# Sparse attention and a squared-ReLU feed-forward on one core: transposing on TensorE instead of in the DMA queues

## The chip, the cores and the metric

The kernel runs on one core of a Trainium2 chip. The metric is the device time of one execution in microseconds; the time of before is the median of three runs.

## The reference

Inputs are `q`, `k`, `v` of 8 batches x 8 heads x 576 tokens x 64, all float32, and two weights. Cut to what matters:

```python
scores = (q @ k.transpose(0, 1, 3, 2)) / sqrt(64)
rel = pos[:, None] - pos[None, :]
mask_local   = (rel >= 0) & (rel < 32)                    # heads 0 to 3
mask_strided = (rel >= 0) & (pos_k % 32 == pos_q % 32)    # heads 4 to 7
attn = softmax(where(mask, scores, -1e9))
x = (attn @ v).transpose(0, 2, 1, 3).reshape(4608, 512)
h = x @ w_in                                              # 512 -> 2048
g = s * relu(h)**2 + b
out = g @ w_out                                           # 2048 -> 512, float32
```

## The kernel before, in words

**Attention.** Heads are worked on in pairs: a batch `b` has four pairs `m`, 0 and 1 of the band (local) heads, 2 and 3 of the strided ones. A pair stands on the 128 partitions as two heads of 64. Band heads are cut in `LT` = 6 tiles of `LQ` = 96 queries, each with a window of 128 keys. Strided heads are cut by residue in `ST` = 8 groups of `SQ` = 72 tokens. For each pair `pair_steps` makes these steps: transposes of queries and keys (`trans`, L527 and L535), so that the 64 features lie on partitions; scores (`score`, L656); exponentials on ACT and a mask on DVE; the product with the values (`av`, L717), whose last column gives the sum; a division on DVE into `x_nat`; and a transpose of the outputs (`xtrans`, L764) into `xT`, from which the feed-forward reads.

Transposes are made in two ways. On TensorE a transpose is a matmul against the identity into a PSUM bank, and ACT or DVE copies the bank out (all these copies are recorded at L437, `copy_on`). In batches 0 and 1 (`HEAD_T` = 2) the band heads are transposed singly (L527): two matmuls of 64 columns of weights, one head into PSUM partitions 0 to 63, the other into 64 to 127. In batches 2 to 4 `pair_post` first copies two heads of the loaded queries or keys next to each other (`qp`, `kp`), and one matmul of 128 columns of weights (L535) takes both. Strided heads lie side by side as loaded and always go as a pair. The other way is a transposing DMA on SP's queue: strided keys from batch 3 (`k_dma`), band keys from `KB_DMA` = 4, strided queries from `QS_DMA` = 3, band queries from `QB_DMA` = 5 (`q_dma`; `q_spread` then copies the queries apart), band outputs from batch 2 (`x_dma`), strided outputs from `XS_DMA` = 4 through a buffer in DRAM (`x_out`, `x_in`).

**Feed-forward.** The 4608 tokens are cut in 9 blocks `T` of 512. `ff1` (L1016) multiplies a block with `w_in`; ACT takes the ReLU, ACT or DVE the square. `ff2` (L1271) multiplies with `w_out`. From block 2 on the second product is done with seven instead of eight block products (`ff2_seven`, L984), in the last two blocks the first one too (`ff1_seven`, L1241). `L1526` is filler that keeps TensorE running in the head.

**Order.** The order on every engine is written out when the program is made. `Plan` keeps a clock in ns. A `Step` on TensorE has a reckoned cost (`ns`: 40 for a position of single heads, 35 for another transpose or an `av`, 216 for a 512-column matmul), keys that it needs, and work that it posts to ACT, DVE, POOL or the queues. `flush` picks among posted work by the time at which it was ready plus a priority from `ORDER`, which here has four sets, changed at the times in `UNTIL`. The main loop takes an attention step when it is ready and due, else a step of `ff1` or `ff2`.

**Banks.** PSUM has eight banks: `t` (transposes, 1), `s` (scores, 2), `a` (attention outputs, 1), `f1` and `f2` (feed-forward, 2 each). `group_of` says which banks a fill may take; from batch `KB_DMA` on, `a` may also use `t`.

**Loads.** `fetch_qk(b)` has POOL issue the loads of queries and keys of a batch, `fetch_v(b)` those of the values. In `fetch_qk` POOL first copies one element of the transposed strided keys of batch b-1 to `gate` (L1356), so that it waits until that transposing DMA has landed. From `QB_DMA` and `KB_DMA` on band queries and keys are loaded head by head (L387). `landing` reckons when a load will be there.

Of the kernel before, what the change touches and what calls it, by code (L numbers as in the profile page):

```python
# [139 lines left out]
class Step:  # L140
    def __init__(self, fn, ns, needs=(), group=None, keys=(), posts=(), after=None):
# [4 lines left out]
UNTIL = (26000.0, 110000.0, 215000.0)  # L146
ORDER = [
    {"g": 0.0, "S": -2500.0, "in": 500.0, "w_mix": 2500.0, "wc": 0.0, "ev": 2500.0, "c21": -200.0,
     "c11": 2500.0, "c12": 200.0, "C22": 1500.0, "fv": -200.0, "Vb": 0.0, "x": 500.0, "Ub": 500.0,
     "xc": 500.0, "fe": -400.0, "k": -400.0, "fu": 200.0, "Va": 500.0, "p": 1000.0, "c22": -800.0,  # L150
     "Ua": -200.0, "e": -1500.0, "q": 500.0, "r": -800.0, "u": -2500.0, "SLACK": 200.0,
     "ahead": 0.0, "p2": -800.0, "r3": 500.0, "inkl0": 2500.0, "q3": 1000.0, "lead": 0.9,
     "r1": 2500.0, "k2": 2500.0, "x0": 0.0, "invs0": -400.0, "x2": 1500.0, "k0": 200.0,
     "inql1": 1000.0, "k3": -200.0, "q0": 1000.0, "q2": 2500.0, "p3": 2500.0, "inql0": 200.0,
     "r0": -2500.0, "invs1": 200.0, "p0": -1500.0, "r2": -200.0, "invl1": -2500.0, "x3": -200.0,
     "q1": 2500.0, "invl0": 2500.0, "k1": 0.0, "inkl1": -1500.0, "p1": 1000.0, "x1": 2500.0},
    {"g": -1500.0, "S": -400.0, "in": 2500.0, "w_mix": 200.0, "wc": -800.0, "ev": -200.0,
     "c21": 2500.0, "c11": -1500.0, "c12": -2500.0, "C22": 1500.0, "fv": -1500.0, "Vb": 2500.0,
     "x": 0.0, "Ub": 500.0, "xc": 200.0, "fe": 500.0, "k": -800.0, "fu": 1000.0, "Va": 500.0,
     "p": -200.0, "c22": 0.0, "Ua": 2500.0, "e": -1500.0, "q": -2500.0, "r": 1500.0, "u": -2500.0,  # L160
     "SLACK": 600.0, "ahead": -0.2, "r3": -200.0, "k1": 1500.0, "q1": -200.0, "invl1": -800.0,
     "x2": -800.0, "x3": -2500.0, "lead": 1.1, "k3": 0.0, "p1": 0.0, "inql0": 2500.0,
     "r0": -1500.0, "r2": -400.0, "invs0": 1000.0, "k0": -400.0, "q3": 0.0, "invl0": 1500.0,
     "p2": 2500.0, "x1": 500.0, "invs1": -200.0, "inkl0": 500.0, "inql1": 0.0, "q0": 1500.0,
     "k2": -2500.0, "inkl1": -2500.0, "p0": 500.0, "q2": -200.0, "p3": 0.0, "x0": 1000.0,
     "r1": -2500.0},
    {"g": 1500.0, "S": 2500.0, "in": 500.0, "w_mix": -800.0, "wc": 1000.0, "ev": 1000.0,
     "c21": -1500.0, "c11": 2500.0, "c12": 1000.0, "C22": 1000.0, "fv": -1500.0, "Vb": -200.0,
     "x": -400.0, "Ub": 200.0, "xc": -1500.0, "fe": -1500.0, "k": 500.0, "fu": 2500.0,
     "Va": 500.0, "p": 200.0, "c22": 200.0, "Ua": -400.0, "e": 1500.0, "q": 1000.0, "r": 1500.0,  # L170
     "u": 1500.0, "SLACK": 600.0, "ahead": -0.05, "lead": 1.1, "k1": -400.0, "inkl0": -400.0,
     "p2": 2500.0, "q0": 1000.0, "inql1": 1500.0, "x0": -200.0, "inql0": 2500.0, "q3": 1000.0,
     "invs0": 1000.0, "invl1": -800.0, "p0": 200.0, "k0": -1500.0, "r1": 1000.0, "inkl1": 0.0,
     "k3": 1000.0, "q1": -1500.0, "x2": -400.0, "invs1": 0.0, "x1": 200.0, "x3": 1000.0,
     "p3": 200.0, "p1": 2500.0, "k2": -400.0, "r3": 2500.0, "r2": 1500.0, "invl0": 1500.0,
     "q2": 1500.0, "r0": 2500.0},
    {"g": 200.0, "S": 200.0, "in": 200.0, "w_mix": 200.0, "wc": 1500.0, "ev": 1500.0,
     "c21": -400.0, "c11": -2500.0, "c12": -400.0, "C22": 200.0, "fv": -400.0, "Vb": -200.0,
     "x": -1500.0, "Ub": -400.0, "xc": 0.0, "fe": 0.0, "k": -200.0, "fu": -2500.0, "Va": -200.0,
     "p": -1500.0, "c22": 200.0, "Ua": 0.0, "e": -200.0, "q": 2500.0, "r": 200.0, "u": -1500.0,  # L180
     "SLACK": 1000.0, "ahead": -0.05, "q0": 1500.0, "q1": 500.0, "invs1": -400.0, "x1": -800.0,
     "q3": -400.0, "p2": -2500.0, "q2": 2500.0, "p1": -800.0, "p3": 0.0, "k1": -2500.0,
     "r2": -1500.0, "x3": -800.0, "inql1": 500.0, "invl1": -400.0, "x0": 1500.0, "inkl1": 500.0,
     "inkl0": 200.0, "inql0": -1500.0, "k0": 200.0, "r3": -2500.0, "r1": -2500.0, "k3": -1500.0,
     "invl0": -1500.0, "x2": -2500.0, "invs0": -2500.0, "k2": 200.0, "lead": 0.9, "p0": 1500.0,
     "r0": -2500.0},
]
# [34 lines left out]
def lay_out(ctx, tc, nc, q, k, v, moe_w_in, moe_w_out, moe_s, moe_b, out, order, q_shape, out_shape,  # L222
# [15 lines left out]
    SQ, ST = 72, 8  # L238
# [77 lines left out]
    QB_DMA, KB_DMA, QS_DMA, XS_DMA = 5, 4, 3, 4  # L316
    x_dram = [tc.dram_tile([S, 128], FP16, name=f"x_dram{i}") for i in range(4)]
# [52 lines left out]
    paired = {}  # L370

    def load_qk(b):
# [7 lines left out]
        for name, src in (("q", q), ("k", k)) if b else ():  # L380
            tl = inp.tile([LQ, NL], FP16, tag=name + "l", name=name + "l")
            loaded[b, name + "l"] = tl
            if b >= (QB_DMA if name == "q" else KB_DMA):

                dst = tl.rearrange("p (m t e d) -> p m e t d", m=2, t=LT, e=2)
                for h in range(4):
                    nc.gpsimd.dma_start(out=dst[:, h // 2, h % 2],  # L387
                                        in_=src[b, h].rearrange("(t p) d -> p t d", p=LQ))
            else:
                nc.gpsimd.dma_start(out=h4(tl), in_=view_l(src, b))  # L390
        for name, src in (("q", q), ("k", k)):
            if name == "k":
                ts = ks[b % 2]
            elif b < QS_DMA + 2:
                ts = inp.tile([SR, NS], FP16, tag="qs", name="qs")
            else:
                ts = loaded[b - 2, "qs"]
            if name == "k" and b in (2, 3) or name == "q" and b in (QS_DMA, QS_DMA + 1):
                nc.sync.dma_start(out=ts[SQ:SR], in_=h_zero.ap())
            load_s(ts, src, b)  # L400
            loaded[b, name + "s"] = ts
# [37 lines left out]
    def pair_post(b, name, mm, key):  # L439

        if (b, name) not in paired:
            paired[b, name] = None

        def g(eng):
            if paired[b, name] is None:
                paired[b, name] = inp.tile([128, 2, LT, 2 * D], FP16, tag="pp", bufs=3,
                                           name=name + "p")[0:LQ]
            from_ = loaded[b, name + "l"]
            copy_on(eng, out=paired[b, name][:, mm].rearrange("p j (e d) -> p e j d", e=2),
                    in_=from_.rearrange("p (m e j d) -> p m e j d", m=2, e=2, d=D)[:, mm])  # L450
        plan.post([key], {"A": 810, "V": 350}, g,
                  [("in", name + "l", b, mm)])

# [26 lines left out]
    HEAD_T = 2  # L480
    PE_MASK = 1
# [4 lines left out]
    def group_of(kind, b, m, q=False):  # L486
# [5 lines left out]
        elif b == 1 and kind == "a":  # L492
            banks = f1 + a
        elif b >= KB_DMA and kind == "a":
            banks = a + t
        elif b == 1 and q:
            banks = t + f2
        elif b == 2 and q:
            banks = t + f1
        elif kind == "t" and b == 1:  # L500
            banks = t + f1 + a
# [5 lines left out]
    def pair_steps(b, m):  # L507
# [10 lines left out]
        def trans(name, j, group):  # L518
            alone = loc and b < HEAD_T

            def f():
                if j == 0:
                    st["p" + name] = bank(group).bitcast(FP16)[:, 0:S]
                if alone:
                    for e in range(2):
# [7 lines left out]
                src = (paired[b, name][:, mm, j] if loc else  # L533
                       loaded[b, name + sfx][0:SQ, 1024 * mm + j * 128:1024 * mm + j * 128 + 128])
# [40 lines left out]
        k_by_dma = b >= (KB_DMA if loc else 3)  # L575
        q_by_dma = b >= (QB_DMA if loc else QS_DMA)
        x_by_dma = b >= 2 if loc else XS_DMA <= b

        def k_dma(eng):
            if loc:  # L580
                st["k"] = kT_loc[mm]
                if b > KB_DMA and (b - KB_DMA) % 2:

                    if b == KB_DMA + 1:
                        loaded["kT", mm] = qkp.tile([128, ST * SR], FP16, tag="kTs", name="kT_alt")
                        nc.gpsimd.memset(loaded["kT", mm][:, 0:LPAD], 0.0)
                    st["k"] = loaded["kT", mm]
                nc.sync.dma_start_transpose(
                    out=st["k"][:, LPAD:LPAD + S].rearrange("d (t p) -> d t p", t=nt),
                    in_=loaded[b, "kl"][:, 768 * mm:768 * mm + 768])  # L590
                return
            if b < KB_DMA:
                st["k"] = qkp.tile([128, ST, SR], FP16, tag="kTs", name="kTs")
            else:
                if (b, "kT2") not in loaded:
                    loaded[b, "kT2"] = inp.tile([128, 2, ST, SR], FP16, tag="vs", name="kT2")
                st["k"] = loaded[b, "kT2"][:, mm]
# [1040 lines left out]
```

## Time and profile before

| | |
|---|---|
| median of three runs | 297.5 us (297.36 to 298.87) |
| profiled execution, its own time | 297.4 us |
| span of its instructions | 295.5 us |
| TensorE (PE) busy, matmuls | 289.5 us, 2803 |
| weight loads (PEld) busy | 219.3 us |
| DVE busy | 236.8 us |
| ACT busy | 194.6 us |
| POOL busy | 92.8 us |
| mean DMA rate | 129 GB/s |
| granted TensorE clock | 1.000 |

Busy is the time in which at least one instruction of the engine is under way. A matmul's record is longer than the distance to the next start, since matmuls are pipelined: what a matmul costs a full TensorE is read from start to start. In a line of the timeline the columns are start and length in us, engine, line, operation, out<-in, `weights rows*columns`, shape of the output and type, and how many instructions are merged. In a line of the stages each engine has its busy time and, in brackets, its instructions; then come the granted clock, the DMA share and GB/s.

### The profile page before, as it was taken

The page shows a single profiled execution, that of the slowest core. Times are in us where ns is not written, and L with a number is a line of the kernel's source. Part 1 is how long each engine was busy: PE and PEld are TensorE (multiplying, and loading weights), DVE is VectorE, ACT ScalarE, POOL GpSimd, SP SyncE. Part 2 cuts the span into 40 slices and gives each one's busy share as a digit, 9 for nine tenths or more (in the row PEclk, how much of TensorE's full clock was granted, in tenths as well). Part 3 has the DMA queues.
Part 4 walks back from the last instruction along what each step waited for, and adds up shares of the span by engine and source line. Part 5 has one row for each costly group of instructions (what it writes and reads, how often), then busy time and mean ns, then how long its engine had stood idle before and what let it go on. Part 6 is the DMA issues. An engine that isn't in the chain of part 4 may idle for free.

```text
span 295.5 us, 7106 instructions
## 1 busy us (share of the span) xinstructions
PE 289.5 (98%) x2803; PEld 219.3 (74%) x2803; DVE 236.8 (80%) x498; ACT 194.6 (66%) x334; POOL 92.8 (31%) x140
## 2 busy tenths in 40 slices
PE   7899999999999999999999999999999999999995
PEld 3775655665565567989867785779888999999984
DVE  5765977888976789768986888688899689888874
ACT  3667855897967797947873777478966564576500
POOL 8872623610961396008820195200002000000000
PEclk9999999999999999999999999999999999999999
DMA  8999999999999699979999999998430300210314
GB/s 131 180 206 203 213 184 174 208 189 128 140 160 145 98 91 161 160 138 146 162 149 147 169 168 130 134 137 213 44 104 13 109 35 2 71 38 0 109 39 143
DMA packets 106152, 38.19 MB, mean 129 GB/s; under 512 B 85414, under 2 KB 103974, under 8 KB 106118
## 3 DMA queue, kind: packets, MB, share of 16 engines
q0 software_dynamic: 60848, 18.23, 64.2%
q1 hardware_dynamic: 45270, 19.51, 36.1%
q8 instruction: 22, 0.36, 0.5%
q14 instruction: 12, 0.10, 0.1%
HBM read 36.99 MB, written 10.62 MB: 161 GB/s over the span
## 4 chain that ended last, share of the span: by engine, by line
PE 95%; POOL 3%; DVE 1%; issue 1%; ACT 0%; POOLq 0%
PE ps_f L1016 32%; PE ps_f L984 25%; PE ps_f L1271 8%; PE ps_s L656 5%; PE ps_f L1241 3%; PE ps_a L717 3%; PE ps_t L1241 2%; PE ps_s L984 2%; PE ps_a L1241 2%; PE ps_s L1241 2%; PE ps_t L717 1%; PE ps_t L984 1%; PE ps_s L1271 1%; PE ps_f L717 1%; PE ps_t L535 1%; PE ps_f L535 1%
## 5 line engine op out<-in xcount | busy, mean ns | idle before, releaser
L1016 PE MATMUL ps_f<-xT,w_in_sb 128*128 128x512 f16 (+4 forms) x568 | 115.3, 331 | 0.0
L1042 ACT ACTIVATE u<-ps_f 128x512 f16<-128x512 f32 x107 | 62.8, 595 | 34.5 <-PE ps_f L1016 32.4
L1016 PEld LDWEIGHTS <-w_in_sb 128*128 128x128 f16 x576 | 57.1, 114 | 23.1
L984 PEld LDWEIGHTS <-gT 128*128 128x128 f16 x608 | 58.3, 98 | 8.6
L984 PE MATMUL ps_f<-w_out_sb,gT 128*128 128x256 f16 x376 | 53.4, 273 | 0.0
L1271 PE MATMUL ps_f<-w_out_sb,gT 128*128 128x512 f16 x112 | 31.9, 379 | 0.0
L674 ACT ACTIVATE p_str<-ps_s 72x432 f16<-72x432 f32 (+1 forms) x45 | 21.1, 488 | 10.1 <-PE ps_s L656 9.5
L1052 DVE TENSOR_TENSOR gT<-u 128x1024 f16<-128x1024 f16 x32 | 21.8, 682 | 5.2 <-ACT u L1042 4.8
L1050 ACT ACTIVATE gT<-u 128x1024 f16<-128x1024 f16 x24 | 25.4, 1058 | 0.7
L984 PE MATMUL ps_f<-w_mix,gT 128*128 128x256 f16 x176 | 24.9, 273 | 0.0
L674 ACT ACTIVATE p_loc<-ps_s 128x384 f16<-128x384 f32 x46 | 20.7, 489 | 5.5 <-PE ps_s L656 5.1
L744 DVE TENSOR_TENSOR x_nat<-ps_a,rec 72x384 f16<-72x384 f32 (+2 forms) x45 | 23.5, 523 | 0.7
L852 DVE TENSOR_TENSOR gT<-gT 128x1024 f16<-128x1024 f16 x34 | 22.4, 683 | 0.3 <-ACT gT L1050 0.3
L415 POOL DMA_DIRECT2D v_loc<-in_v_dram x24 | 17.8, 767 | 10.1 <-DMA w_out_sb<-in_moe_w_out_dram 4.2
L984 PEld LDWEIGHTS <-S 128*128 128x128 f16 x176 | 17.1, 98 | 2.7
L717 PEld LDWEIGHTS <-p_str 72*128 72x128 f16 x256 | 13.6, 98 | 5.8 <-ACT p_str L674 0.7
L420 POOL DMA_DIRECT2D v_str<-in_v_dram x16 | 13.0, 817 | 12.8 <-PE ps_f L1016 3.7
L1271 PEld LDWEIGHTS <-gT 128*128 128x128 f16 x128 | 11.4, 98 | 6.9 <-issue 0.2
L1356 POOL COPY gate<-kT 1x1 f16<-1x1 f16 x6 | 2.2, 371 | 45.0 <-DMA kT<-ks 45.0
L984 PE MATMUL ps_f<-w_mix,S 128*128 128x256 f16 x112 | 15.0, 273 | 0.0
L734 DVE RECIPROCAL rec<-ps_a 72x6 f32<-72x6 f32 (+2 forms) x45 | 8.3, 184 | 8.4 <-PE ps_a L717 8.0
L717 PEld LDWEIGHTS <-p_loc 128*128 128x128 f16 x192 | 11.2, 98 | 5.0 <-ACT kTs L437 0.8
(235 smaller groups left out, 543.1 us busy)
## 6 DMA issues: line engine op xcount, KB each, us to landing
out_dram<-o SPq DMA_DIRECT2D x34, 256.0 KB
w_in_sb<-in_moe_w_in_dram POOLq DMA_DIRECT2D x4, 512.0 KB, 9.9
w_out_sb<-in_moe_w_out_dram POOLq DMA_DIRECT2D x4, 512.0 KB, 10.7
qs<-in_q_dram POOLq DMA_DIRECT2D x6, 288.0 KB, 8.1
ks<-in_k_dram POOLq DMA_DIRECT2D x6, 288.0 KB, 9.9
v_loc<-in_v_dram POOLq DMA_DIRECT2D x24, 72.0 KB, 9.8
ql<-in_q_dram POOLq DMA_DIRECT2D x4, 288.0 KB, 9.9
kl<-in_k_dram POOLq DMA_DIRECT2D x16, 72.0 KB, 3.7
```

The source lines that it names most:

```text
L415: nc.gpsimd.dma_start(out=vl[LPAD:128, h, :, 0:D], in_=v_band(b, h))
L674: nc.scalar.activation(out=st["pw", g][0:nk, 0:2 * n * nq], in_=st["s", g][0:nk, 0:2 * n * nq], func=AF.Exp, scale=scale)
L717: nc.tensor.matmul(out=st["pa", g][:, n % 6, :], lhsT=st["pw", gp_][0:nk, i * nq:i * nq + WIDE], rhs=vt[0:nk, 2 * mm + e, j, :])
L744: nc.vector.tensor_tensor(out=x_at(0, cnt), in0=st["pa", g][0:nq, 0:cnt, 0:D], in1=st["rec", g][0:nq, 0:cnt].to_broadcast([nq, cnt, D]), o ...
L852: {"V": nc.vector, "P": nc.gpsimd}[eng].tensor_tensor(out=at(out), in0=at(x), in1=at(y), op=op)
L984: nc.tensor.matmul(out=gts[name, T, t][:, 0] if halves else gts[name, T][:, t], lhsT=lhs(k, t), rhs=rhs(k), start=fresh and k == 0 and (ha ...
L1016: nc.tensor.matmul(out=gts["h", T, ft][:, lo:hi], lhsT=w_in_sb[ft // 4][:, ct].rearrange("p (x l) -> p l x", l=4)[:, ft % 4], rhs=xT[ct][: ...
L1042: nc.scalar.activation(out=u, in_=gts["h", T, ft], func=AF.Relu)
L1050: nc.scalar.activation(out=g, in_=u, func=AF.Square)
L1052: nc.vector.tensor_tensor(out=g, in0=u, in1=u, op=ALU.mult)
L1241: nc.tensor.matmul(out=st[bk][:, 256 * t:256 * t + 256], lhsT=lhs(t, c), rhs=rhs(c), start=fresh and t == c == 0, stop=t == c == 1, skip_g ...
L1271: nc.tensor.matmul(out=gts[id_], lhsT=gts[T][:, ft, ts * 128:(ts + 1) * 128], rhs=w_out_sb[:, ft, cols], start=(ft == 0), stop=(ft == NFT ...
```

## The change

All queries, keys and outputs of all batches are transposed on TensorE, band heads always singly. `pair_post` and all transposing DMAs go, with the buffer in DRAM and the zeros that filled the padding. Loads of batch b+2 are posted when batch b's queries and keys are copied out; they wait no more for the keys of batch b+1, and the copies to `gate` go. Band queries and keys are always loaded for four heads at once. `a` may use `t` from batch 2. `landing` reckons 2.6 us instead of 6.0 us after 60 us. `ORDER` now has 48 sets, which change every few microseconds; the set of the first 26 us is the old one.

```diff
-UNTIL = (26000.0, 110000.0, 215000.0)
-ORDER = [
...
+CHANGES = (
+    (0.0, {"g": 0.0, "S": -2500.0, "in": 500.0, "w_mix": 2500.0, "wc": 0.0, "ev": 2500.0,
...
+UNTIL = tuple(at for at, _ in CHANGES[1:])
+ORDER = [{k: v for _, c in CHANGES[:n + 1] for k, v in c.items()} for n in range(len(CHANGES))]
...
-    QB_DMA, KB_DMA, QS_DMA, XS_DMA = 5, 4, 3, 4
-    x_dram = [tc.dram_tile([S, 128], FP16, name=f"x_dram{i}") for i in range(4)]
...
-            if b >= (QB_DMA if name == "q" else KB_DMA):
-
-                dst = tl.rearrange("p (m t e d) -> p m e t d", m=2, t=LT, e=2)
-                for h in range(4):
-                    nc.gpsimd.dma_start(out=dst[:, h // 2, h % 2],
-                                        in_=src[b, h].rearrange("(t p) d -> p t d", p=LQ))
-            else:
-                nc.gpsimd.dma_start(out=h4(tl), in_=view_l(src, b))
+            nc.gpsimd.dma_start(out=h4(tl), in_=view_l(src, b))
...
-    def pair_post(b, name, mm, key):
...
+    WIDE_A = True
...
-        elif b >= KB_DMA and kind == "a":
+        elif b >= 2 and kind == "a" and WIDE_A:
             banks = a + t
...
-            alone = loc and b < HEAD_T
+            alone = loc
...
-                src = (paired[b, name][:, mm, j] if loc else
-                       loaded[b, name + sfx][0:SQ, 1024 * mm + j * 128:1024 * mm + j * 128 + 128])
+                src = loaded[b, name + sfx][0:SQ, 1024 * mm + j * 128:1024 * mm + j * 128 + 128]
...
-        k_by_dma = b >= (KB_DMA if loc else 3)
-        q_by_dma = b >= (QB_DMA if loc else QS_DMA)
-        x_by_dma = b >= 2 if loc else XS_DMA <= b
-
-        def k_dma(eng):
...
-        def q_dma(eng):
...
-        def q_spread(eng):
...
         for name in ("q", "k"):
-            if (k_by_dma if name == "k" else q_by_dma):
-                continue
             gr = group_of("t", b, m, True)
...
-        def x_out(eng):
...
-        def x_in(eng):
...
-        def x_dma(eng):
...
-        if x_by_dma and loc:
...
-        else:
-            gr = group_of("t", b, m)
-            for j in range(nt):
-                steps.append(xtrans(j, gr))
+        gr = group_of("t", b, m)
+        for j in range(nt):
+            steps.append(xtrans(j, gr))
...
-        return ring + (6000.0 if plan.t > 60000.0 else 1600.0 if plan.t > 14000.0 else 600.0)
+        return ring + (2600.0 if plan.t > 60000.0 else 1600.0 if plan.t > 14000.0 else 600.0)
...
     def fetch_qk(b):
-        for mm in range(2):
-            if (b - 1, "kTs", mm) in loaded:
-
-                nc.gpsimd.tensor_copy(out=gate[0:1, 2 + mm:3 + mm],
-                                      in_=loaded[b - 1, "kTs", mm][0:1, 0, 0:1])
         load_qk(b)
...
-                        [("soon" if b > 1 else "k", (b + 1 if b > 1 else b, mk)) for mk in range(2, 4)],
-                        {"P": 2900.0 + (2200.0 if b + 2 >= QB_DMA else 0.0)},
+                        [],
+                        {"P": 2900.0},
                         lambda eng, b=b: fetch_qk(b + 2), [("fetch", b + 2)])
```

## The prediction

> **What bounds the kernel now.** I read the page first (busy shares, the slices, the chain), then the busy time by stage, then TensorE's waits, and last the timeline of the few places where the kernel already does on TensorE what the change makes it do everywhere.
>
> ```profile
> span 295.5 us, 7106 instructions
> PE 289.5 (98%) x2803; PEld 219.3 (74%) x2803; DVE 236.8 (80%) x498; ACT 194.6 (66%) x334; POOL 92.8 (31%) x140
> PEclk9999999999999999999999999999999999999999
> PE 95%; POOL 3%; DVE 1%; issue 1%; ACT 0%; POOLq 0%
> ...
> L1356 POOL COPY gate<-kT 1x1 f16<-1x1 f16 x6 | 2.2, 371 | 45.0 <-DMA kT<-ks 45.0
> ```
>
> TensorE is busy for 289.5 of 295.5 us, at full clock in every slice, and is 95% of the chain that ends last. A busy TensorE is not yet one at its peak, so the chain must be looked at in pieces (start, length, what):
>
> ```profile
> 23.38 4.96 PE ps_f L1016 x23
> ...
> 281.88 3.49 PE ps_f L984 x32
> ```
>
> 4.96/23 is 216 ns for each 512-column matmul, 3.49/32 is 109 ns for each of 256 columns: 2.35 to 2.37 columns per ns from one start to the next, early and late. The matmuls follow each other at full rate. The stages (PE busy is the second number):
>
> ```profile
> 50.00:100.00 50.00, 50.00 (x452) 30.04 (x451) 41.10 (x90) 40.27 (x75) 19.69 (x29) 1.00 1.42 159
> 150.00:200.00 50.00, 50.00 (x416) 36.40 (x414) 40.08 (x82) 31.96 (x53) 15.03 (x21) 1.00 1.52 145
> 200.00:250.00 50.00, 50.00 (x508) 44.62 (x507) 43.53 (x91) 34.24 (x53) 1.65 (x1) 1.00 0.32 76
> ```
>
> From 50 us on TensorE has no idle time, and in the list of its waits none stands after 50 us (its weight load has one of 0.3 us there); the ones of the whole run are
>
> ```profile
> PE ps_t L527 <- DMA ql<-in_q_dram: 0.9, 1, 0.9
> PE ps_s L1521 <- PEq L1622: 0.8, 1, 0.8
> PE ps_f L717 <- DVE v_loc L437: 0.7, 1, 0.7
> PE ps_f L717 <- POOL v_loc L437: 0.4, 1, 0.4
> ```
>
> all in the head. So no DMA, transposing or not, holds TensorE up after the head, and whatever is added to TensorE after it adds its issue time to the end. POOL's 45.0 us wait for the transposed keys is idle time of an engine that nobody waits for.
>
> **The change part by part.** In the compiled order, TensorE's matmuls grow from 2801 to 3325; nothing but transposes changes in number. I price them from start to start, not by a record's duration (about 0.2 us, mostly pipeline):
>
> ```profile
> 51.48 0.42 PE L535 MATMUL ps_f<-ident,qp 96*128 96x96 f16 x6
> 51.74 1.03 PE L1271 MATMUL ps_s<-w_out_sb,gT 128*128 128x512 f16 x4
> ...
> 55.52 0.42 PE L535 MATMUL ps_t<-ident,qs 72*128 72x72 f16 x8
> 55.78 0.38 PE L1271 MATMUL ps_f<-w_out_sb,gT 128*128 128x512 f16 x1
> ...
> 28.27 0.45 PE L527 MATMUL ps_t<-ident,ql 96*64 96x96 f16 x12
> 28.65 0.62 PE L1016 MATMUL ps_f<-xT,w_in_sb 128*128 128x512 f16 x2
> 29.20 0.45 PE L527 MATMUL ps_f<-ident,ql 96*64 96x96 f16 x12
> ...
> 31.43 0.45 PE L527 MATMUL ps_t<-ident,kl 96*64 96x96 f16 x12
> 31.71 0.42 PE L527 MATMUL ps_f<-ident,kl 96*64 96x96 f16 x12
> 32.06 1.05 PE L1016 MATMUL ps_f<-xT,w_in_sb 128*128 128x512 f16 x4
> ```
>
> A 96-column transpose of a head pair takes 0.26/6 = 43 ns; a 72-column one 0.26/8 = 32.5 ns. Of single heads (L527), 12 in one run take 0.38 us (28.27 to 28.65) and 24 take 0.63 us (31.43 to 32.06): 0.25 us for the six further positions, 42 ns for two heads together. Side by side they cost what a pair costs.
>
> (1) Band queries and keys, 96 columns: 8 batches x 2 pairs x 2 x 6 = 192 positions after; 108 before (48 of single heads in batches 0 and 1, 60 paired). 84 x 42.5 ns = 3.6 us. (2) Strided queries and keys: 256 after, 96 before; 160 x 32.5 ns = 5.2 us. (3) Band outputs: 96 after, 24 before; 72 x 42.5 ns = 3.1 us. (4) Strided outputs: 128 after, 64 before; 64 x 32.5 ns = 2.1 us. Sum 14.0 us.
>
> (5) **Going into and out of single heads.** The same lines show a price that is paid per run, not per transpose. A run of 12 holds 6 positions, 0.25 us, but takes 0.38: 0.13 too much. The two L1016 between the runs take 28.65 to 29.20, 0.55 instead of 2 x 0.216 = 0.43: 0.12 too much. Together 0.25; with the finer starts of the trace I find 0.24 (0.22 to 0.24 by the neighbour's width). The paired transposes at 51.48 have no such excess. The Trainium skill, TensorEngine Tiling, section Key Properties, says two things here: tiles of the array work in parallel, and a change of tiling mode drains TensorE. By the first alone the change costs 14.0 us; the second gives no figure, so I take the trace's. In the compiled order the single heads stand in 8 unbroken runs before and 41 after (24 of them of 12; nine are of 2, a single position between other matmuls). 33 x 0.24 = 7.9 us.
>
> Sum on TensorE: 14.0 + 7.9 = 21.9 us.
>
> (6) The end of these fills: copies out of PSUM. DVE gains 8 band query copies at 754 ns (6.0 us), 18 strided ones at 455 (8.2), 10 of outputs at 457 to 757 (about 6), 3 of strided keys at 448 and one of band keys at 757 (2.1), and loses 10 spreads at 302 and 10 at 386 (6.9); the rest nets to about nothing: about +15, 252 us. ACT gains 14 key copies at about 0.64, 6 query copies at 0.633 and 10 output copies at 0.637 (19 us) and loses 2 + 8 spreads, 4 pairing copies at 0.83, 2 squares at 1.06 and 2 row copies (13 us): about +6, 200 us. Of a span of 320 that is 79% and 63%, as before: beside TensorE's work, priced at nothing. If the cover fails it shows as a TensorE wait, which is the second rival.
>
> (7) Moved and removed: 50 transposing DMAs, 8 stores to x_dram and 4 zero fills leave SP's queue, which then issues only outputs; POOL loses 8 gate copies and 21 load issues (28 per-head loads become 7 whole ones). The loads of batch b+2 no longer stand behind the landing of b+1's strided keys, so they issue sooner. All this feeds buffers for which TensorE did not wait after the head: nothing gained. Cost if wrong: `landing` now reckons 2.6 us after the queue where it reckoned 6.0; a load issued two batches ahead has some 30 us.
>
> (8) Priorities. The first 398 matmuls stand in the same order in both kernels (to 35.95 us in this trace), so the head and its waits stay. Behind it every wait is new. Bounds: below, nothing can be regained, since there is no wait after 50 us; from above, the `t` bank. Each batch fills it 12 times, a fill and its copy take 1 to 1.9 us by the rows above, about 16 us of the 33 us that a batch has in the new order, so it is half taken, and band and strided outputs (`a`) may now use it from batch 2. I bound new waits by 0 and 8 us and take 0.5, near the nearest row: in the 30 us of 20 to 50, where batch 1 is transposed wholly on TensorE, PE is busy for 30.00.
>
> Total: the profiled execution took 297.4 us, 2 us over its span, against a median of 297.5. 297.5 + 21.9 + 0.5 = 320 us.
>
> **The rivals.**
>
> A, likeliest (0.74): as summed, 320, with 316 to 324 for runs and waits a little off.
>
> B, late copies (0.16): the score matmuls stand, by the intervals above, about 0.9 us behind the last key transpose in the new order, about the time of the pipeline and one copy (0.2 + 0.64). If queues on DVE and ACT make each wait 0.1 us for some 70 of the new fills, 7 us come on top: 327. Against it: batch 0 to 2 of the present kernel are ordered as tightly and TensorE does not wait after 50 us; and the order reckons single heads without the price of (5), so on the chip TensorE runs later than planned and the copies have more time.
>
> C, the switches are cheaper (0.07): if part of the 0.24 us is absorbed, most likely in the runs of 2, down to 297.5 + 14.0 = 311.5. Against it: the run of 4 in the head pays it too.
>
> D, not slower (0.03): the added transposes would have to vanish in TensorE's stream. That is so only if the long matmuls include waiting: it decides from where 21.9 us are regained over 245 us, so that a 512-column matmul comes every 197 ns instead of 216. Waits for the transposing DMAs would be such a reserve; TensorE shows none. It would give 297.5 or less. "The change doesn't do what it says" has no room: the counts are those of the compiled order.
>
> **How the numbers follow.** Predicted is A: 320. The range takes A whole, the upper part of C and B up to 328: 315 to 328; left out are most of C, the tail of B, and D, about 0.17. A measurement of this kernel can tell about 0.5% (1.5 us) from no change. D is the only case that is not slower: faster 0.01, same 0.02, slower 0.97.
>
> **What would show it.** Right: TensorE's busy share stays at 97% or more, its list of waits stays empty after 50 us, single-head runs each carry about 0.24 us of excess, DMA's busy share falls below half in the stages from 50 to 200, POOL's gate wait is gone. Wrong: waits of TensorE or of its weight load for DVE or ACT copies of `qD`, `kT` or `xT` (then B); L1016 starts at 216 ns right behind a single head (then C); a time under 305 us would mean that TensorE was not the bound.

## The result and the profile after

| kernel | median | runs | ratio to before, 95% interval |
|---|---|---|---|
| before | 297.75 us | 4 | |
| changed | 320.69 us (320.6 to 320.88) | 4 | 1.0765 [1.0734, 1.0795] |

The ratios use the fast runs alone; of all runs in this document one is slow, the fourth of `a_dma2` (334.69 us, over 1.5% above its fastest), and without it the median of that kernel is 330.01 us.

The change costs 22.9 us; 22.5 were predicted. (The kernel before has one run more here than ahead of the prediction, so its median moved from 297.5 to 297.75 us.) The profiled execution took 320.63 us. From its page:

```profile
span 318.7 us, 8004 instructions
PE 311.9 (98%) x3327; PEld 233.3 (73%) x3327; DVE 247.4 (78%) x515; ACT 199.0 (62%) x348; POOL 71.6 (22%) x106
PEclk9999999999999999999999999999999999999999
PE 92%; DVE 3%; POOL 3%; issue 1%; ACT 0%; DVEq 0%; POOLq 0%
```

The picture is that of before, 23.2 us longer: TensorE 98% busy at full clock, some 520 more matmuls, DVE and ACT with smaller shares than before. The stages (PE is the first engine; the last three numbers are the granted clock, the DMA share and GB/s):

```profile
50.00:100.00 50.00, 50.00 (x493) 29.34 (x491) 39.52 (x86) 35.44 (x64) 16.11 (x22) 1.00 1.09 122
150.00:200.00 50.00, 50.00 (x530) 35.02 (x529) 36.51 (x71) 36.56 (x64) 8.98 (x12) 1.00 0.54 68
200.00:250.00 50.00, 50.00 (x602) 40.72 (x600) 40.90 (x89) 32.27 (x56) 0.00 (x0) 1.00 0.10 33
250.00:300.00 50.00, 48.87 (x454) 46.15 (x453) 45.73 (x81) 29.71 (x45) 0.00 (x0) 1.00 0.11 38
```

The queue of the loads (q0) keeps its bytes, SP's queue (q1) loses half of them and most of its time (packets, MB, share of the span of 16 engines; before, then after):

```profile
q0 software_dynamic: 60848, 18.23, 64.2%
q1 hardware_dynamic: 45270, 19.51, 36.1%
```

```profile
q0 software_dynamic: 47072, 18.23, 53.9%
q1 hardware_dynamic: 10422, 9.90, 9.5%
```

From 20 to 250 us TensorE is as full as it was; after that 1.1 us are missing. Two lines of the waits of TensorE and of its weight load (us in total, times, longest) matter:

```profile
PE ps_s L1514 <- DVE qD_loc L1389: 1.1, 1, 1.1
...
PEld L886 <- issue: 9.2, 33, 0.7
```

The first line is those 1.1 us, TensorE's only wait behind the head. The second is not a wait for anybody: 33 times the weight load stands idle before a single head (L886 is the former L527) although nothing that the profile knows holds it. Where that goes is seen in the timeline, at a place where single positions stand between 256-column matmuls:

```profile
212.81 0.27 PE L1257 MATMUL ps_f<-w_out_sb,gT 128*128 128x256 f16 x1
213.01 0.23 PE L886 MATMUL ps_t<-ident,ql 96*64 96x96 f16 x2
213.18 0.28 PE L1257 MATMUL ps_f<-w_out_sb,gT 128*128 128x256 f16 x1
213.39 0.23 PE L886 MATMUL ps_t<-ident,ql 96*64 96x96 f16 x2
```

From 213.01 to 213.39 TensorE does one position (0.043) and one 256-column matmul (0.109): 0.15 us of work in 0.38 us. The position takes 0.17, and the matmul ahead of the next position takes 0.21. A run of twelve costs no more:

```profile
150.34 0.59 PE L1289 MATMUL ps_f<-xT,w_in_sb 128*128 128x512 f16 x2
150.87 0.45 PE L886 MATMUL ps_t<-ident,kl 96*64 96x96 f16 x12
151.25 0.62 PE L1289 MATMUL ps_f<-xT,w_in_sb 128*128 128x512 f16 x2
```

Two 512-column matmuls take 0.53 instead of 0.43, six positions 0.38 instead of 0.26, and the next matmul 0.03 more: about 0.24 in all. Away from single heads the long matmuls come as they did before the change (pieces of the chain: start, length, what):

```profile
91.77 1.51 PE ps_f L1289 x7
124.57 1.75 PE ps_f L1257 x16
```

That is 216 ns for each of 512 columns and 109 ns for each of 256.

### The profile page after: what moved, and what is told of

Read it like the earlier page. It is cut to its first block, busy times and chain, and to the rows that moved or that the text cites. A ratio compares the mean times of both kernels' runs of the same rounds, so it can differ in the third digit from the quotient of the medians.

```text
span 318.7 us, 8004 instructions
## 1 busy us (share of the span) xinstructions
PE 311.9 (98%) x3327; PEld 233.3 (73%) x3327; DVE 247.4 (78%) x515; ACT 199.0 (62%) x348; POOL 71.6 (22%) x106
## 3 DMA queue, kind: packets, MB, share of 16 engines
q0 software_dynamic: 47072, 18.23, 53.9%
## 4 chain that ended last, share of the span: by engine, by line
PE 92%; DVE 3%; POOL 3%; issue 1%; ACT 0%; DVEq 0%; POOLq 0%
PE ps_f L1289 30%; PE ps_f L1257 22%; PE ps_f L1544 8%; PE ps_s L953 5%; PE ps_f L1514 3%; PE ps_t L886 3%; PE ps_a L1014 2%; PE ps_t L1061 2%; PE ps_t L893 2%; PE ps_s L1257 2%; PE ps_s L1514 1%; PE ps_a L1514 1%; PE ps_t L1014 1%; PE ps_t L1514 1%; PE ps_s L1544 1%; PE ps_t L1257 1%
## 5 line engine op out<-in xcount | busy, mean ns | idle before, releaser
L1289 PE MATMUL ps_f<-xT,w_in_sb 128*128 128x512 f16 (+4 forms) x568 | 118.9, 332 | 0.0
L1315 ACT ACTIVATE u<-ps_f 128x512 f16<-128x512 f32 x106 | 62.6, 596 | 34.0 <-PE ps_f L1289 33.1
L1257 PEld LDWEIGHTS <-gT 128*128 128x128 f16 x608 | 56.9, 98 | 8.8
L1257 PE MATMUL ps_f<-w_out_sb,gT 128*128 128x256 f16 x376 | 55.4, 273 | 0.0
L1323 ACT ACTIVATE gT<-u 128x1024 f16<-128x1024 f16 x22 | 23.3, 1059 | 0.5
L1125 DVE TENSOR_TENSOR gT<-gT 128x1024 f16<-128x1024 f16 x34 | 22.5, 678 | 0.9 <-PE ps_f L1257 0.8
L1041 DVE TENSOR_TENSOR x_nat<-ps_a,rec 72x384 f16<-72x384 f32 (+2 forms) x42 | 21.4, 511 | 0.7
L810 ACT COPY xT<-ps_t 128x576 f16<-128x576 f16 x17 | 10.8, 637 | 15.4 <-PE ps_t L1061 12.9
L1061 PEld LDWEIGHTS <-x_nat 72*128 72x128 f16 (+1 forms) x224 | 15.3, 98 | 6.3 <-DVE x_nat L1041 0.6
L953 PE MATMUL ps_s<-qD_str,kTs 128*72 128x144 f16 x121 | 17.2, 226 | 0.0
L1061 PE MATMUL ps_t<-ident,x_nat 72*128 72x72 f16 (+1 forms) x190 | 16.8, 200 | 0.0
L1257 PE MATMUL ps_f<-w_mix,S 128*128 128x256 f16 x112 | 16.6, 273 | 0.0
```

What stands on the lines that cost most here:

```text
L953: nc.tensor.matmul(out=st["s", g][0:nk, c:c + 2 * nq], lhsT=(st["k"][:, i * nq:i * nq + nk] if loc else st["k"][:, i, 0:SQ]), rhs=st["q"][ ...
L1041: nc.vector.tensor_tensor(out=x_at(0, cnt), in0=st["pa", g][0:nq, 0:cnt, 0:D], in1=st["rec", g][0:nq, 0:cnt].to_broadcast([nq, cnt, D]), o ...
L1061: nc.tensor.matmul(out=st["px"][:, nq * j:nq * j + nq], lhsT=st["x"][:, j, :], rhs=ident[0:nq, 0:nq], is_transpose=True)
L1125: {"V": nc.vector, "P": nc.gpsimd}[eng].tensor_tensor(out=at(out), in0=at(x), in1=at(y), op=op)
L1257: nc.tensor.matmul(out=gts[name, T, t][:, 0] if halves else gts[name, T][:, t], lhsT=lhs(k, t), rhs=rhs(k), start=fresh and k == 0 and (ha ...
L1289: nc.tensor.matmul(out=gts["h", T, ft][:, lo:hi], lhsT=w_in_sb[ft // 4][:, ct].rearrange("p (x l) -> p l x", l=4)[:, ft % 4], rhs=xT[ct][: ...
```

## The experiments

All are compared with the kernel before on the same chip; its medians were 297.14 us in the first group (`a_wide`, `a_whole`, `b_single`, `b_xpe`), 297.61 in the second (`a_pairload`, `a_dma`, `a_prio`, `b_pair1`) and 297.56 in the third (`a_dma2`, `a_xc2`).

| kernel | median us | ratio to before, 95% interval |
|---|---|---|
| a_wide | 312.61 | 1.0519 [1.0502, 1.0535] |
| a_whole | 332.44 | 1.1185 [1.1154, 1.1215] |
| b_single | 304.96 | 1.0263 [1.0245, 1.0282] |
| b_xpe | 305.51 | 1.0282 [1.0265, 1.0299] |
| a_pairload | 313.46 | 1.0540 [1.0526, 1.0553] |
| a_dma | 336.40 | 1.1308 [1.1279, 1.1336] |
| a_prio | 323.35 | 1.0869 [1.0854, 1.0885] |
| b_pair1 | 300.78 | 1.0109 [1.0086, 1.0132] |
| a_dma2 | 331.57 | 1.1118 [1.1064, 1.1172] |
| a_xc2 | 320.14 | 1.0763 [1.0749, 1.0778] |

**The switch alone, the order kept (a_wide).**

```diff
-                    for e in range(2):
-                        at = ((2 * mm + e) * LT + j) * D
-                        nc.tensor.matmul(
-                            out=st["p" + name][64 * e:64 * e + 64, nq * j:nq * j + nq],
-                            lhsT=loaded[b, name + "l"][:, at:at + D],
-                            rhs=ident[0:nq, 0:nq], is_transpose=True)
+                    at = (2 * mm * LT + j) * D
+                    nc.tensor.matmul(
+                        out=st["p" + name][:, nq * j:nq * j + nq],
+                        lhsT=loaded[b, name + "l"][:, at:at + 2 * D],
+                        rhs=ident[0:nq, 0:nq], is_transpose=True)
```

> The changed kernel in its own order, but each position of two single heads (two 64-column matmuls) is one matmul of 128 neighbouring columns of the loaded tile. It leaves out the transpose of the second head of each pair (the columns taken are those of the first head's next tile); the number of positions, all copies, loads and all other work stay. Theory (a price of 0.24 us per unbroken run of single heads, 41 runs, of which 5 lie in the first 12 us beside other waits): 9 to 10 us less than the changed kernel, 311 to 312 us, and no matmul beside a transpose starts late. Rival (the two halves of a position do not run side by side for free, or the time went to waits): not over 2 us less, 318.5 us or more.

Measured: 312.61 us, 8.1 us under the changed kernel (7.5 when each is taken against its own before); the spans are 310.8 and 318.7, 7.9 apart. The place shown above now reads

```profile
206.80 0.21 PE L885 MATMUL ps_t<-ident,ql 96*128 96x96 f16 x1
206.85 0.27 PE L1256 MATMUL ps_f<-w_out_sb,gT 128*128 128x256 f16 x1
206.96 0.21 PE L885 MATMUL ps_t<-ident,ql 96*128 96x96 f16 x1
```

0.05 + 0.11 = 0.16 us per position and matmul instead of 0.38. The waits on "issue" at this line and the one wait that stays are

```profile
PEld L885 <- issue: 1.3, 2, 1.1
PE ps_s L1513 <- DVE qD_loc L1388: 1.1, 1, 1.1
```

Two instead of 33, and the longer of the two is in the head. So the price belongs to going from the full array to single heads and back; what in TensorE takes the time no trace names. The order on TensorE is the same position for position, so the gain can be read place by place: 8.2 us behind 20 us, where 36 of the 41 runs lie, 0.23 us each. In the first 20 us nothing came back, a_wide is 0.3 us behind there: TensorE waits elsewhere (for `v_loc` on POOL 1.0 us, where it was 0.5, and 0.5 for `w_in_sb`). That is why the gain is 1 to 2 us short of the expectation.

**Fewer runs (a_whole).**

```diff
-            for j in range(nt):
-                steps.append(trans(name, j, gr))
+            parts = [trans(name, j, gr) for j in range(nt)]
+            if loc:
+                s = parts[-1]
+                s.fn = lambda fs=[x.fn for x in parts]: [fn() for fn in fs]
+                s.ns, s.group = sum(x.ns for x in parts), gr
+                parts = [s]
+            steps += parts
```

> The changed kernel, but the six positions of a band fill are one step that nothing can be put between. In the compiled order the runs of single heads fall from 41 to 29, positions and everything else stay in number. Theory of a price per run: 12 x 0.24 = 2.9 us less than the changed kernel, 317.8 us, if the coarser steps bring no new wait. Rival (the price is per position or per transpose): the same as the changed kernel, 320.7 us.

Measured: 332.44 us, and the time says nothing on the price: the condition "no new wait" failed. The priorities were set for other steps, and six steps of a fill made one gave another order of everything behind:

```profile
PE ps_a L1519 <- DVE ks L1377: 2.6, 1, 2.6
PE ps_t L1019 <- DVE x_nat L1046: 2.6, 1, 2.6
PE ps_t L1066 <- DVE x_nat L1046: 2.0, 5, 1.2
PE ps_f L1262 <- DVE Va L1181: 1.8, 2, 1.6
```

and in the stage behind them

```profile
260.00:270.00 10.00, 4.95 (x32) 3.53 (x31) 5.63 (x16) 1.69 (x3) 0.00 (x0) 0.50 0.00 0
```

With one for `qD_loc` of 1.3 us that is about 10 us of waits. The last four of them, of 2.6, 2.6, 1.2 and 1.3 us, begin at 257.1 us, and at the end of the first, at 259.7 us, the clock granted to TensorE falls to half for 10 us (the 0.50 behind POOL's busy time); the other three lie within these 10 us. What the trace still shows is that the runs that are left cost from 0.22 to 0.25 us each from start to start, as before.

**Single heads in the kernel before (b_single).** `HEAD_T` is 8, and `fetch_qk` reckons the loads accordingly.

```diff
-    HEAD_T = 2
+    HEAD_T = 8
```

> The kernel before, but band queries and keys of batches 2 to 4 are transposed as single heads instead of being copied into pairs first; the transposing DMAs stay. Positions stay 108, runs of single heads go from 8 to 27, the pairing copies (about 4 us of ACT and 2 us of DVE) fall away. Theory of a price per run: 19 x 0.24 = 4.6 us more than before, 302.3 us. Rival (single heads are as cheap as pairs and save the copies): 297.7 us or less.

Measured: 304.96 us, 7.8 more than before, where 4.6 were expected for the runs. The rival is out. The other 3 us are new waits behind the altered order, again in the list:

```profile
PE ps_a L717 <- DVE x_nat L744: 1.1, 1, 1.1
PE ps_s L656 <- DMA kT<-ks: 0.3, 1, 0.3
PE ps_s L656 <- ACT p_str L674: 0.2, 1, 0.2
PE ps_f L984 <- DVE Va L903: 0.2, 1, 0.2
```

2.4 us with 0.16 us more for each, and a few too short for the list. (From start to start a wait costs about 0.16 us more than listed, since the record of the matmul ahead of it, 0.27 us for 256 columns, is that much longer than the 0.109 us which it costs in a full stream.) The 19 further runs cost their 4.6 us.

**Outputs on TensorE (b_xpe).**

```diff
-        x_by_dma = b >= 2 if loc else XS_DMA <= b
+        x_by_dma = False
```

> The kernel before, but all attention outputs are transposed on TensorE; queries and keys go as before, with all their transposing DMAs. 72 positions of 96 columns at 42.5 ns and 64 of 72 columns at 32.5 ns are added, no run of single heads. Theory (TensorE is full, what is added to it comes on top): 5.1 us more than before, 302.9 us, and up to 1 us more for waits on the one transposing bank. Rival (the output's way through DRAM and the transposing DMAs cost something that is saved): 300 us or less.

Measured: 305.51 us, 8.4 more than before, over the 5.1 to 6.1 that were expected. Two new waits

```profile
PE ps_f L984 <- DVE Va L903: 1.3, 1, 1.3
PE ps_t L717 <- ACT xT L437: 0.7, 1, 0.7
```

cost 2.4 us from start to start, more than the 1 us that I allowed. Behind 20 us the further transposes take 5.2 us from start to start, without the second of these waits: they come on top as reckoned. Some 0.8 us are in smaller pieces. Nothing is seen to be saved by the DMAs that fell away.

**Pairs by loading (a_pairload).**

```diff
+            if b >= HEAD_T:
+                dst = tl.rearrange("p (m j e d) -> p m e j d", m=2, j=LT, e=2)
+                for h in range(4):
+                    nc.gpsimd.dma_start(out=dst[:, h // 2, h % 2],
+                                        in_=src[b, h].rearrange("(p j) d -> p j d", j=LT))
+            else:
+                nc.gpsimd.dma_start(out=h4(tl), in_=view_l(src, b))
...
-            alone = loc
+            alone = loc and b < HEAD_T
```

> The changed kernel, but from batch 2 on band queries and keys are loaded head by head into the layout of pairs (head pair, tile, head, feature), so that TensorE transposes a pair with one 128-column matmul and no copy is needed. The order of steps stays. Runs of single heads fall from 41 to 8; loads grow from 14 issues of 4 heads to 4 issues each from batch 2 on. Theory (price per run, loads hidden): 33 x 0.24 = 7.9 us less than the changed kernel, 312.5 to 313 us, and no wait of TensorE for a DMA. Rival (loads in smaller pieces come late, or the price is not in the single heads): 316 us or more.

Measured: 313.46 us, 7.2 us under the changed kernel. That is the price per run once more, less one wait for the strided keys at 56 us, which have the smaller loads ahead of them (I expected none):

```profile
PE ps_f L900 <- DMA ks<-in_k_dram: 0.9, 1, 0.9
```

Leaving aside a_wide, which omits part of the work, it is the best of the kernels that make all transposes on TensorE, and still 15.9 us behind the one before.

**The DMA load put back (a_dma, a_dma2).**

```diff
+        def spare_dma(eng, name, n):
+            nc.sync.dma_start_transpose(out=spare[2 * mm + n],
+                                        in_=loaded[b, name + "l"][:, 768 * mm:768 * mm + 768])
+        if loc and b >= 2:
+            for name in ("q", "k"):
+                for n in range(2):
+                    plan.post([("in", name + "l", b, mm)], {"D": 1300.0}, ...)
```

> The changed kernel with 48 transposing DMAs of 96 x 768 put back on SP's queue, from the loaded band queries and keys of batches 2 to 7 into spare tiles that nobody reads. The order on TensorE, DVE and ACT is the changed kernel's. Theory (TensorE waits for no DMA, so relieving the DMA engines gained nothing): the DMA share goes back over 1.0 in the stages from 50 to 200 us and the time stays at 320.7 us within 1 us. Rival (part of the 22 us is net of a gain from the relieved DMA): 3 us or more above the changed kernel.

Measured: 336.40 us, 15.7 over the changed kernel. The DMA share went over 1.0 as expected (1.63, 1.56 and 1.23 in the three stages up to 200 us), but my expectation of the time missed. The loads of values came late, DVE stood idle for them (13.1 us), and TensorE for DVE. Two things could make them late, so the next run keeps the transposing DMAs and takes away the holding back: `in_=still`, a tile that is written once.

> As the run with 48 transposing DMAs added to the changed kernel (336.4 us), but they read a tile that never changes instead of the loaded queries and keys, so no load waits for them; issue times, sizes and SP's queue are the same. If the 15.7 us came from holding back (the load of band keys waits on POOL for the last transposing DMA that reads its tile, 11.7 us once, and the values are queued behind it): within 1.5 us of the changed kernel, 319 to 322 us, and no load of values late. If they came from the sharing of the DMA engines (loads land later whatever they wait for): 330 us or more, with DVE still waiting for v_loc. In between, both have a part.

Measured: 331.57 us, 10.9 over the changed kernel (9.3 by the median of its other three runs, 330.01). The edit did more than was meant: with nothing to wait for, the transposing DMAs are not issued at the same times as in a_dma. The first four, of a_dma and then of a_dma2:

```profile
48.73 7.72 SPq L935 DMA_TRANSPOSE spare<-ql  x4
```

```profile
9.40 8.05 SPq L937 DMA_TRANSPOSE spare<-still  x4
```

In a_dma2 they run in the head, and TensorE has a wait for the queries of batch 1 at 29 us that is not in a_dma (`PE ps_t L889 <- DMA ql<-in_q_dram`, 2.9 us). So the two times can't be subtracted. But the order of the matmuls is the same in all three kernels, and the loss can be read place by place. Behind the first 20 us, a_dma2's profiled execution loses 2.9 us at 29 us and 9.0 us at 81 us, and nothing later; a_dma's loses 2.5 us at 64, 8.5 us at 81 and 2.6 us at 103 to 107 us. The large loss at 81 us is there without any held buffer, and it is the landing that is late: of the values that DVE stands for, the last were issued at 62.6 us and landed 22.6 us later (17.0 in a_dma), where 8.4 us were enough in the changed kernel. So for most of the loss no held buffer is needed; the sharing of the DMA engines with the transposing DMAs is what is left. The issues of the two kernels, the changed one first (count, KB, median us to landing):

```profile
v_loc<-in_v_dram POOLq DMA_DIRECT2D x24, 72.0 KB, 7.7
```

```profile
v_loc<-in_v_dram POOLq DMA_DIRECT2D x24, 72.0 KB, 10.9
```

and in a_dma2's waits of DVE and of TensorE:

```profile
DVE v_loc L813 <- DMA v_loc<-in_v_dram: 8.4, 1, 8.4
...
PE ps_a L1026 <- DVE x_nat L1053: 7.2, 1, 7.2
```

and in the stage that follows

```profile
85.00:92.00 7.00, 3.37 (x19) 1.68 (x19) 4.77 (x15) 0.34 (x1) 2.27 (x3) 0.51 1.44 149
```

One late load of values stands at the head of DVE's queue for 8.4 us; the divisions behind it free no bank; TensorE stands idle for 7.2 us, from 81.4 us on, and has half the clock from 85.2 to 92.0 us, 3.4 us beyond the wait. Whether the held buffers caused a_dma's losses at 64 and at 103 us isn't settled, since the issue times differ too; these two kernels also vary by 3 to 6 us from run to run.

**The old priorities (a_prio).** `CHANGES` and the tables made from it are replaced by the four sets of before.

> The changed kernel with the four sets of priorities of the kernel before, at their times, instead of the 48 new ones. The same instructions in another order from 26 us on; runs of single heads 37 instead of 41. Theory (the transposes cost 22 us whatever the order, and the new priorities only keep waits away that a foreign order brings): 1 us less for the runs, and 3 to 8 us more in waits of TensorE after 50 us, 323 to 328 us. Rival (the new priorities are without worth, or are part of the cost): 320.7 us or less.

Measured: 323.35 us, 2.7 us over the changed kernel, with 37 runs instead of 41. With 1 us less for runs, the new priorities keep away some 3.6 us of waits; they are no part of the cost.

**Batch 1 in pairs (b_pair1).** The same load layout as in a_pairload, for batch 1 in the kernel before.

> The kernel before, but band queries and keys of batch 1 are loaded head by head into the layout of pairs and transposed as pairs; batch 0 stays single, all else and the order stay. Runs of single heads fall from 8 to 5, the three that go (243 ns each) lie where TensorE is full. Theory: 0.7 us less than before, 296.4 us. Rival (the loads of batch 1, in smaller pieces and with 6 more issues on POOL ahead of the weights for the second product, come late in the busiest part of the DMA queues): the same or 1 to 4 us more.

Measured: 300.78 us, 3.2 more. The three runs are gone from the trace, and from 28 to 36 us TensorE gains the 0.7 us that they were reckoned at. But two waits that were not there follow, `PE ps_f L1277 <- DMA w_out_sb<-in_moe_w_out_dram`, 0.5 us at 38 us, and `PE ps_f L723 <- ACT v_loc L442`, 0.4 us at 49 us; smaller pieces come with them, and 0.9 us are lost behind the last matmul. The profiled execution took 299.31 us, the least of the six, so the rest of the 3.2 us isn't settled. It is the rival's side.

**The one wait behind the head (a_xc2).**

```diff
+ORDER[40]["xc"] = -1500.0
```

> The changed kernel with one number of one set of priorities altered (xc in the set from 246 us), which puts four sums of xT ahead of one square's difference and one eviction on DVE at 254 us. Theory (TensorE's one wait behind 50 us, 1.1 us and with the restart 1.3 us, is for those sums standing at DVE's end of the queue): the wait goes or falls under 0.3 us and the time falls by 1.0 to 1.4 us against the changed kernel, to about 319.4 us. Rival (the eviction that is now later is waited for in its place): within 0.5 us of the changed kernel.

Measured: 320.14 us; against the changed kernel 0.55 us less, 0.36 when each is taken against its own before. In the changed kernel the square's difference (L1125) and the eviction (L1176) stood ahead of the four sums of `xT` (L1389):

```profile
254.99 0.68 DVE L1125 TENSOR_TENSOR gT<-gT 128x1024 f16<-128x1024 f16 x1
255.62 0.75 DVE L1176 SCALAR_TENSOR_TENSOR Va<-ps_f,sb_all,bcs 128x512 f32<-128x512 f32 x1
256.28 0.28 DVE L1389 TENSOR_TENSOR qD_loc<-xT,xT 128x256 f16<-128x256 f16 x1
256.48 0.28 DVE L1389 TENSOR_TENSOR qD_loc<-xT,qD_loc 128x256 f16<-128x256 f16 x1
256.82 0.49 PE L1514 MATMUL ps_s<-qD_loc,ks 128*128 128x256 f16 x3 [1.13 <-DVE qD_loc L1389]
```

Now the sums (L1390) come first,

```profile
255.00 0.28 DVE L1390 TENSOR_TENSOR qD_loc<-xT,xT 128x256 f16<-128x256 f16 x1
255.20 0.28 DVE L1390 TENSOR_TENSOR qD_loc<-xT,qD_loc 128x256 f16<-128x256 f16 x1
...
255.81 0.74 DVE L1177 SCALAR_TENSOR_TENSOR Va<-ps_f,sb_all,bcs 128x512 f32<-128x512 f32 x1
```

and the 1.1 us wait is gone, but TensorE now waits 0.2 us for `v_str` and 0.2 us for the copy `U`: about half came back at once.

## Why the prediction was right

Spans add up best, since they belong to single executions: 318.7 - 295.5 = 23.2 us.

1. *Positions, (1) to (4), 14.0 us.* Added up from start to start behind 20 us in the two traces, the 224 further strided transposes take 7.3 us and the 156 further positions of 96 columns, without the price of (5), 6.7: 14.0. a_wide has the same positions and no single heads: 310.8 - 295.5 = 15.3 us, of which 1.3 are the wait that it shares with the changed kernel. That 14.0 are left there too is in part chance, since a_wide also lacks the three runs that before has behind the head (0.7 us). b_xpe shows the outputs' part to come on top alone.
2. *In and out of single heads, (5), 7.9 us.* From start to start the 36 runs behind 20 us cost 8.4 us, 0.23 each; three of them stand in before too, and the 33 that were added cost 7.7. The counted runs and the 0.24 us of the trace of before were the right measure. The gap of the spans between the changed kernel and a_wide, 318.7 - 310.8 = 7.9, is the same number for another count: all 41 runs, less what was lost in the head. a_pairload, which drops just the 33, and b_single show the price from two sides.
3. *Copies, (6), nothing.* DVE has 247.4 and ACT 199.0 us, reckoned 252 and 200. TensorE's own list has no wait for a copy out of the `t` bank behind the head, and its weight loads wait 0.3 us for copies of strided keys there. The cover held in the order that was made for it; in b_xpe and b_single, with other orders, copies, divisions and evictions were late by 2 to 3 us.
4. *DMA relief, (7), nothing gained.* Right for the sum, which closes without it. But what I said of the cost was too easy. The changed order needs the relief, as a_dma and a_dma2 show. And the DMA share did not fall below half in the stages from 50 to 200 us (1.09, 0.83 and 0.54): the loads alone fill that much, since they keep their bytes and 53.9% of the engines' span, nearly all of it before 200 us (the last load is issued at 184 us, 187 before). The transposing DMAs that left are 54 in the trace of before, not 50.
5. *New waits, (8), 0.5 us.* Mis-sized: 1.3 us, 1.1 listed; the sign that TensorE's list stays empty behind 50 us failed by this one wait. It is not at the `t` bank, but at 255 us, where attention, whose last product with the values now starts at 249.8 instead of 214.9 us, releases the tiles for the sums of the weights, and DVE has these and the sums of `xT` to do at once.

14.0 + 7.7 + 1.3 = 23.0 of the 23.2 us.

Of the rivals, B (late copies) and C (cheaper switches) are not seen in the changed kernel: 1.3 us is all the waiting that was added, and its runs of two pay the full price. D (not slower) falls: a 512-column matmul still comes every 216 ns.

## What to carry to other kernels

When the timeline shows TensorE starting matmuls at full rate and its list of waits is empty, price an added matmul from start to start at its nearest twin in the trace, and count also how often the order goes in and out of a narrower shape: here that was a third of the cost. An engine that waits for no DMA gains nothing from fewer DMAs, but an order made for an empty queue may need it empty. A change of steps under priorities set for other steps cost waits of 2 to 4 us in b_single, b_xpe and a_prio and of about 10 us in a_whole; take those from the list of waits before reading the difference as the price of the change.

## What the runs showed of the hardware

- A run of single heads costs 0.22 to 0.25 us whether it holds 1 or 12 positions (the 36 runs behind 20 us in the changed kernel): mostly 0.09 us at the end of the matmul before it (up to 0.12), 0.12 within, 0.01 to 0.03 at the next start.
- A late load can cost more than its wait. In a_dma2 TensorE was granted half its clock from 85.2 to 92.0 us: that began 3.8 us into a wait of 7.2 us and went on for 3.4 us after it. In a_whole it was half from 259.7 to 270.0 us, from the end of a wait of 2.6 us on. A wait of 2.9 us at 29 us in a_dma2 left the clock full, so the length of the wait alone didn't decide.
- With 48 transposing DMAs on SP's queue beside them, loads of values of 72 KB landed after a median of 10.9 us (a_dma2) instead of 7.7 us (changed kernel), the slowest of those shown above after 22.6 us.
